# The input product of the last batch: four of eight pairs of ff tiles by seven block products, seeded and summed through PSUM

## The chip, the cores and the metric

The kernel runs on one core of one Trainium2 chip. The metric is the device time of one execution in microseconds (us); the time of the kernel before is the median of three executions. A core has five engines with instruction streams of their own: TensorE (PE in the profile, with its weight loads as PEld), VectorE (DVE), ScalarE (ACT), GpSimd (POOL) and SyncE (SP, which here only issues transfers). Matmuls read on-chip memory (SBUF) and write PSUM, which has eight banks of 512 fp32 columns for each of 128 partitions.

## What is computed

A block-sparse attention, whose output is the input of a two-layer network with a sigmoid-approximated gelu between the layers:

```python
def _moe_ref(x, w_in, w_out):
    h = x @ w_in                                  # [3072, 512] @ [512, 2048]
    g = h * (1.0 / (1.0 + np.exp(-1.702 * h)))
    return (g @ w_out).astype(np.float32)         # [3072, 2048] @ [2048, 512]

def reference(**kwargs):
    ...
    attn_out = _attn_ref(**attn_kwargs)           # 4 batches, 8 heads, 768 positions, 64 wide
    x = attn_out.transpose(0, 2, 1, 3).reshape(B * S, H * D)
    return _moe_ref(x=x, **moe_kwargs)
```

The change concerns `h = x @ w_in` and the gelu of the last batch only.

## The kernel before

A batch of 768 tokens is worked as two *units* of 384 tokens (`HALF`). Unit `u` of batch `b` is `2*b` or `2*b + 1`; the last batch (`b = 3`) has units 6 and 7. The hidden dimension of 2048 is 16 *ff tiles* of 128 (`NT = 16`), and `NI = 8` pairs of them. For each ff tile the input product takes four matmuls (`KO = 4` pieces of the 512-wide contraction) into a PSUM bank, and ACT writes the gelu of it to `gT`.

All operations of an engine are kept in program order by a wrapper (`_Ordered`), so an operation that waits holds up all later ones of its engine.

```python
psb = ctx.enter_context(tc.tile_pool(name="psb", bufs=2, space=bass.MemoryType.PSUM))   # tag "big": 2 x 2 banks
pmm = ctx.enter_context(tc.tile_pool(name="pmm", bufs=4, space=bass.MemoryType.PSUM))   # tag "mm": 4 x 1 bank
...
xTT = [[keep.tile([128, 2, HALF], F16, name=f"xT{m}{g}") for g in range(2)] for m in range(2)]
xT = [[xTT[m][p // 2][:, p % 2] for p in range(NP)] for m in range(2)]
gT = [keep.tile([128, NT, HALF], F16, name=f"gT{s}") for s in range(2)]
...
def ff_in(u, nts):
    phs = [pmm.tile([128, HALF], F32, name="ph", tag="mm") for nt in nts]
    for k0 in (0, 2):
        for nt, ph in zip(nts, phs):
            for ko in (k0, k0 + 1):
                pe.matmul(out=ph, lhsT=w_in_sb[:, ko, nt * 128:(nt + 1) * 128],
                          rhs=xT[u % 2][ko], start=(ko == 0), stop=(ko == KO - 1))
    for nt, ph in zip(nts, phs):
        act.activation(out=gT[u % 2][:, nt, :], in_=ph, func=ACT.Gelu_apprx_sigmoid)
```

The output product `g @ w_out` of a batch already uses seven products in place of eight, on pairs of token tiles: pair a is two token tiles of the first unit, b is one of each unit, c is two of the second. `sums` makes the sums of quarters that the seven products need; it reads and updates `gT` on DVE, for pairs `i0` to `i1` of ff tiles.

```python
def sums(self, i0, i1):                      # in class Pair
    i = slice(i0, i1)
    dve.tensor_add(self.s1[:, i], self.a21[:, i], self.a22[:, i])
    dve.tensor_sub(self.s2[:, i], self.s1[:, i], self.a11[:, i])
    dve.tensor_sub(self.a21[:, i], self.a11[:, i], self.a21[:, i])

def p1(self, eng=dve):
    self.x = bank("px")                      # bank(): a tile of pmm, tag "mm"
    product(self.x, self.a11, ts["b11"], True)
    self.t1 = held(self.x, eng)
def p6(self):
    product(self.x, self.s2, ts["t2"], False)
    self.t2 = held(self.x, act)
    dve.tensor_sub(self.s2, self.a12, self.s2)
def p7(self):
    self.w = bank("pw")
    product(self.w, self.a21, ts["t3"], True)
def p2(self):
    y = bank("py")
    product(y, self.a12, ts["b21"], True)
    dve.tensor_add(self.osb(0)[:, 0:DH], y[:, 0:DH], self.t1)
    self.store(0, 0, False)
# ... p3, p4, p5 in the same manner
order = ["a7", "a2", "a6", "b1", "a5", "b7", "a3", "a4", "b6", "b2", "b5",
         "c1", "b3", "c7", "c6", "c2", "c5", "b4", "c3", "c4"]
```

The end of the loop over batches (cut to what the last batch does):

```python
for b in range(1, B):
    n, s = b + 1, (b + 1) % 2
    more = n < B
    u = 2 * b
    # ... pairs a, b, c
    first, second = {}, {0: [lambda: pairs["a"].sums(0, NI)]}
    for nt, i0, i1 in ((7, 0, 4), (13, 4, 7)):
        second[nt] = [lambda i0=i0, i1=i1: pairs["b"].sums(i0, i1),
                      lambda i0=i0, i1=i1: pairs["c"].sums(i0, i1)]
    # ... what the earlier batches do beside the input product
    for w, todo in ((u, first), (u + 1, second)):
        ff_in(w, range(3))
        for nt in range(NT):
            if nt > 2:
                ff_in(w, (nt,))
            for f in todo.get(nt, ()):
                f()
    pairs["a"].p1(act)
    # ...
    for m in "bc":
        pairs[m].sums(NI - 1, NI)
    for what in order:
        getattr(pairs[what[0]], "p" + what[1])()
        # ... attention of the next batch between, if there is one
```

Of the kernel before, what the change touches and what calls it, by code (L numbers as in the profile page):

```python
# [9 lines left out]
F32 = mybir.dt.float32  # L10
BF16 = mybir.dt.bfloat16
F16 = mybir.dt.float16
AX = mybir.AxisListType
ALU = mybir.AluOpType
ACT = mybir.ActivationFunctionType
# [20 lines left out]
def kernel(  # L36
# [10 lines left out]
    B, H, S, D = q.shape  # L47
# [10 lines left out]
    KO = d_model // 128  # L58
    NT = d_ff // 128
    HALF = S // 2  # L60
# [3 lines left out]
    pe = _Ordered(tc, nc.tensor)  # L64
    dve = _Ordered(tc, nc.vector)
    act = _Ordered(tc, nc.scalar)
# [5 lines left out]
    stage = ctx.enter_context(tc.tile_pool(name="stage", bufs=1))  # L72
    castp2 = ctx.enter_context(tc.tile_pool(name="cast2", bufs=1))
    attp = ctx.enter_context(tc.tile_pool(name="att", bufs=4))
    outp = ctx.enter_context(tc.tile_pool(name="outp", bufs=4))
    psb = ctx.enter_context(tc.tile_pool(name="psb", bufs=2, space=bass.MemoryType.PSUM))
    pmm = ctx.enter_context(tc.tile_pool(name="pmm", bufs=4, space=bass.MemoryType.PSUM))
# [3 lines left out]
    raw, early = {}, {}  # L81
# [60 lines left out]
    def v_odd(b):  # L142
        for p in range(NP):
            r = rows_of(b % 2, p)
            dve.tensor_copy(out=r[:, :, 1], in_=r[:, :, 0])
# [87 lines left out]
# [3 lines that stand above are left out]
    w_in_sb = keep.tile([128, KO, d_ff], F16, name="w_in_sb")  # L236
# [38 lines left out]
    def copy(eng, out, in_):  # L275
        if eng is act:
            act.activation(out=out, in_=in_, func=ACT.Copy)
        elif eng == "dve_alone":

            dve.tensor_reduce(out=out, in_=in_.unsqueeze(len(in_.shape)), axis=AX.X, op=ALU.max)  # L280
        else:
            eng.tensor_copy(out=out, in_=in_)
# [58 lines left out]
    def block_sums():  # L341
        for g in range(4):
            dve.tensor_copy(out=vs[0:32, 2 * g:2 * g + 2, 0:D],
                            in_=vs_ps[0][32 * g:32 * g + 32, :]
                            .rearrange("p (h d) -> p h d", d=D))


    def halo_dmas(w5, j0):
        halo_odd(w5, j0)
        halo_even(w5, j0)  # L350
# [220 lines left out]
    def tk(p, s):  # L571
        ps = trans(rows["k", 1][:, p].rearrange("p j h d -> p j (h d)"))
        copy(dve, at(flat_kx(p, s), 0, [[256, NJ], [192, 2], [1, 64]]),
             ps.rearrange("p (j e c) -> p j e c", e=2, c=64))
        ks = attp.tile([128, nb], BF16, name="ks", tag="ks")
        dve.tensor_reduce(out=ks, in_=ps.rearrange("p (n s) -> p n s", s=block),
                          axis=AX.X, op=ALU.max)
        key_halos(p, s)
        key_rows(p, s, ks)
# [3 lines left out]
    def xk(g, b):  # L583
        s = b % 2
        k4 = kxs[s].rearrange("p i (j e) c -> p (i j) e c", e=2)
        src = rows["k", b][:, 2 * g:2 * g + 2].rearrange("p i j h d -> p (i j h d)")
        for e in range(2):
            sp.dma_start(out=k4[:, 2 * g * NJ:2 * (g + 1) * NJ, e, e * 64:e * 64 + 64],
                         in_=src[e * 64:e * 64 + 64], transpose=True)
# [7 lines left out]
    def rest_k(p, s):  # L597
        ks = attp.tile([128, nb], BF16, name="ks", tag="ks")
        dve.tensor_reduce(out=ks.rearrange("p (j e n) -> p j e n", e=2, n=2),
                          in_=at(flat_kx(p, s), 0, [[256, NJ], [192, 2], [block, 2], [1, block]]),  # L600
                          axis=AX.X, op=ALU.max)
        key_halos(p, s)
        key_rows(p, s, ks)
# [4 lines left out]
    a_sb, x_sb, x2 = {}, {}, {}  # L608
# [11 lines left out]
    def values(b, half, g, big=False):  # L620

        pvs = []
        for i in range(2):
            p = 2 * g + i
            a = a_sb[p]
            if big and i == 0:
                ps = psb.tile([128, 1024], F32, name="ps_av", tag="big")
            one = (ps[:, i * 512:i * 512 + 512] if big else
                   pmm.tile([128, 512], F32, name="ps_av", tag="mm"))
            pv = one[:, 0:390].rearrange("p (h j c) -> p h j c", h=2, j=JH)  # L630
            pvs.append(pv)
            for hh in range(2):
                for j in range(JH):
                    for e in range(2):
                        t = 2 * j + e
                        pe.matmul(out=pv[e * 64:e * 64 + 64, hh, j, :], lhsT=a[:, hh, t, :],
                                  rhs=vw[b % 2][:, half * TH + t, 2 * p + hh, 0:D + 1],
                                  start=True, stop=True, skip_group_check=True)
        x2[g] = attp.tile([128, 2, JH, 2, D], F16, name="x2", tag="x2")
        for i in range(2):  # L640
            norm(x2[g][:, i], pvs[i])
# [15 lines left out]
    def dx(g, m):  # L657
        sp.dma_start(out=xTT[m][g].rearrange("p i (j c) -> p (i j) c", c=128),
                     in_=x2[g].rearrange("p i j h d -> p (i j h d)"), transpose=True)
# [17 lines left out]
    def ff_first(p):  # L677
# [6 lines left out]
        if len(seen) == KO:  # L684
            for nt in range(N0):
                act.activation(out=gT[0][:, nt, :], in_=ph0[nt], func=ACT.Gelu_apprx_sigmoid)

    po_now = {}

    def ff_out(u, ms, part):  # L690
# [12 lines left out]
    NI, DH = NT // 2, d_model // 2  # L703
# [265 lines left out]
    for u in range(2):  # L969
        todo = {}  # L970
# [3 lines left out]
        else:  # L974
            def value_rows():
# [7 lines left out]
            todo = {0: [lambda: tk(0, 1)], 3: [lambda: tk(1, 1)], 5: [lambda: v_odd(1)],  # L983
                    6: [lambda: tk(2, 1)], 9: [value_rows], 11: [lambda: tk(3, 1)]}
# [45 lines left out]
# [3 lines that stand above are left out]
        ss = stage.tile([128, NP - 1, 2, NI, 128], F16, name="ss", tag="vf")  # L1033
        u = 2 * b
        pairs = {"a": Pair((u, 0), (u, 1), ss[:, 0], not more),
                 "b": Pair((u, 2), (u + 1, 2), ss[:, 1], not more),
                 "c": Pair((u + 1, 0), (u + 1, 1), ss[:, 2], not more)}
# [4 lines that stand above are left out]
        if b == 1:  # L1042
            first = {0: [lambda: values(1, 1, 0, True)], 2: [lambda: dx(0, 1), lambda: values(1, 1, 1, True)],
                     4: [lambda: dx(1, 1)]}
        elif more:
            for g in range(2):
                xk(g, n)
        if more:
            first.setdefault(6, []).append(lambda: v_odd(n))
            at_k = [(first, 3), (first, 5), (first, 8), (first, 10)] if b == 1 else \  # L1050
                [(first, 8), (first, 10), (first, 12), (first, 14)]
            for p, (when, nt) in enumerate(at_k):
                when.setdefault(nt, []).append(lambda p=p: rest_k(p, s))

            def bring():
                w5 = vw[s].rearrange("p (j e) h c -> p j e h c", e=2)
                vsum(s, range(NJ))
                block_sums()
                halo_dmas(w5, 0)
                sum_dmas(w5, 0)  # L1060

            def later():
                pool.tensor_copy(out=after, in_=ss[:, 2, 0, 0, 0:2])
                load_kc(n + 1)
                load_vc(n + 1)
                load_qc(n + 1)

            if n + 1 < B:
                second[7].append(later)
            when = 7 if b == 1 else 14  # L1070
            first.setdefault(when, []).append(lambda: [xq(g, n) for g in range(2)])
            first.setdefault(9 if b == 1 else 15, []).append(bring)
        for w, todo in ((u, first), (u + 1, second)):
            ff_in(w, range(3))
            for nt in range(NT):
                if nt > 2:
                    ff_in(w, (nt,))
                for f in todo.get(nt, ()):
                    f()
        pairs["a"].p1(act)  # L1080
        if more:
            exp_soon()
        for m in "bc":
            pairs[m].sums(NI - 1, NI)
        for what in order:
            getattr(pairs[what[0]], "p" + what[1])()
            if more:
                for it in meet.get(what, ()):
                    attend(n, it)
# [30 lines left out]
```

## Time and profile before

| | |
|---|---|
| device time | 212.51 us (211.75 to 213.37) |
| span of the profiled execution | 210.6 us |
| mean granted TensorE clock | 1.000 |
| input products, all batches | 512 matmuls of 384 columns, 86.2 us |
| gelus, all batches | 128 on ACT, 60.9 us, mean 490 ns |
| input product of the last batch | 168.10 to 188.90 us |
| output products of the last batch | from 188.90 us, the last begins at 206.37 |

In the timeline each line is a run of like instructions: start and length in us, engine, operation, what it writes and reads, how many; in brackets how long the engine stood idle before it, and whose end released it. `ph` is a bank of the input product, `px`, `pw` and `py` are banks of the output product, `ss` the sums. All operations go through one helper, so they all have its line number, and groups are told apart by the names of their tiles. A table of windows gives, for each stretch of time, its length, the busy time of PE, PEld, DVE, ACT and POOL with the number of instructions, the granted clock, the share of the transfer engines and GB/s.

### The profile page before, as it was taken

The numbers are of one execution on the slowest core, as the hardware profiler recorded it, in microseconds if no ns is written. First come the engines' busy times: TensorE is split into PE (matmuls) and PEld (weight loads), VectorE is DVE, ScalarE is ACT, GpSimd is POOL, SyncE is SP. The second block draws the span as 40 slices with busy tenths as digits, with TensorE's granted clock in tenths as the row PEclk, the third lists the DMA queues.
The fourth block names the chain that finished last, engine by engine and source line by source line (L and its number), as shares of the span: only waits on it lengthen the run. The fifth ranks groups of instructions, "written<-read, shape, count | busy, mean of one in ns | idle before, by whom it ended". The sixth has DMA issues, their size and how long they took to land.

```text
span 210.6 us, 5499 instructions
## 1 busy us (share of the span) xinstructions
PE 201.3 (96%) x2193; PEld 137.1 (65%) x2193; DVE 133.0 (63%) x394; ACT 122.0 (58%) x228; POOL 95.0 (45%) x173
## 2 busy tenths in 40 slices
PE   7879999999999999989999989999999999999993
PEld 2667565556665666556888856557888856668882
DVE  6487956587946669936767860797757710366332
ACT  2674878156685488667744557677444667772220
POOL 8788989699897943425998120220000000000000
PEclk9999999999999999999999999999999999999999
DMA  5999999999998999999999999995043250000223
GB/s 160 302 159 205 241 244 221 175 152 224 167 136 164 131 113 211 157 142 122 167 132 200 177 214 157 174 98 63 3 137 90 72 155 0 3 0 25 84 77 117
DMA packets 96609, 29.33 MB, mean 139 GB/s; under 512 B 84480, under 2 KB 93600, under 8 KB 96584
## 3 DMA queue, kind: packets, MB, share of 16 engines
q0 software_dynamic: 67920, 14.88, 81.9%
q1 hardware_dynamic: 28664, 14.11, 34.2%
q8 instruction: 17, 0.28, 0.6%
q14 instruction: 8, 0.07, 0.1%
HBM read 27.26 MB, written 6.29 MB: 159 GB/s over the span
## 4 chain that ended last, share of the span: by engine, by line
PE 81%; DMA 10%; DVE 3%; POOL 2%; issue 1%; SPq 0%
PE ph L28 36%; PE px L28 14%; PE po L28 10%; DMA xT<-x 8%; PE pw L28 7%; PE ps_av L28 4%; PE py L28 3%; PE ps_s L28 3%; DMA kf<-in_k_dram 2%; POOL vb L28 2%; DVE qT L28 1%; PE ps_t L28 1%; PE ps_x L28 1%; PE ps_q L28 1%; DVE x_sb L28 1%
## 5 line engine op out<-in xcount | busy, mean ns | idle before, releaser
L28 PE MATMUL ph<-xT,w_in_sb 128*128 128x384 f16 x512 | 86.2, 326 | 1.6 <-DMA xT<-x 1.5
L28 ACT ACTIVATE gT<-ph 128x384 f16<-128x384 f32 x128 | 60.9, 490 | 27.2 <-PE ph L28 27.0
L28 PEld LDWEIGHTS <-w_in_sb 128*128 128x128 f16 x512 | 49.4, 98 | 34.0 <-issue 2.2
L28 PEld LDWEIGHTS <-gT 128*128 128x128 f16 x384 | 35.6, 98 | 12.4
L28 ACT ACTIVATE a_sb<-ps_s 128x768 bf16<-128x768 f32 x28 | 21.2, 806 | 11.6 <-PE ps_s L28 11.6
L28 PE MATMUL po<-w_out_sb,gT 128*128 128x512 f16 x96 | 23.1, 380 | 0.0
L28 PEld LDWEIGHTS <-ss 128*128 128x128 f16 x216 | 21.0, 98 | 2.5
L28 DVE TENSOR_TENSOR a_sb<-a_sb,mk 128x768 bf16<-128x768 bf16 x28 | 15.6, 557 | 10.0 <-ACT a_sb L28 8.4
L28 DVE TENSOR_TENSOR ss<-gT 128x512 f16<-128x512 f16 (+3 forms) x21 | 8.0, 381 | 21.4 <-ACT gT L28 21.4
L28 ACT ACTIVATE t<-px 128x256 f32<-128x256 f32 x21 | 8.1, 384 | 20.2 <-PE px L28 20.2
L28 PE MATMUL pw<-tb,gT 128*128 128x256 f16 x144 | 18.7, 273 | 0.0
L28 PE MATMUL px<-ta,ss 128*128 128x256 f16 x144 | 18.7, 273 | 0.0
L28 DVE TENSOR_REDUCE ks<-kx 128x24 bf16<-128x768 bf16 x12 | 11.3, 944 | 7.9 <-DMA kx<-kb 7.9
L28 DVE TENSOR_TENSOR x<-ps_av,rc 128x384 f16<-128x384 f32 x28 | 15.6, 558 | 1.0
L28 POOL DMA_DIRECT2D vw<-in_v_dram x18 | 15.9, 938 | 0.3 <-DMA kq<-in_k_dram 0.3
L28 POOL DMA_DIRECT2D vw<-vw x12 | 6.8, 585 | 19.9 <-DVE vw L28 10.2
L28 POOL DMA_DIRECT2D kb<-in_k_dram x16 | 13.2, 863 | 2.0 <-DMA w_out_sb<-in_moe_w_out_dram 1.6
L28 POOL DMA_DIRECT2D qb<-in_q_dram x16 | 13.3, 914 | 1.0 <-DMA vw<-in_v_dram 1.0
L28 DVE TENSOR_TENSOR osb<-pw,t 128x256 f32<-128x256 f32 x18 | 7.6, 423 | 9.2 <-PE pw L28 5.1
L28 ACT ACT_TABLE_LOAD x10 | 12.8, 1283 | 1.0 <-PEq L1104 0.8
L28 ACT ACTIVATE osb<-px 128x256 f32<-128x256 f32 x9 | 3.4, 379 | 12.0 <-PE px L28 12.0
L28 DVE RECIPROCAL rc<-ps_av 128x6 f32<-128x6 f32 x32 | 6.0, 188 | 6.6 <-PE ps_av L28 6.3
(103 smaller groups left out, 253.7 us busy)
## 6 DMA issues: line engine op xcount, KB each, us to landing
out_dram<-osb SPq DMA_DIRECT2D x18, 256.0 KB, 5.2
vw<-in_v_dram POOLq DMA_DIRECT2D x18, 128.0 KB, 6.0
w_in_sb<-in_moe_w_in_dram POOLq DMA_DIRECT2D x4, 512.0 KB, 8.5
w_out_sb<-in_moe_w_out_dram POOLq DMA_DIRECT2D x4, 512.0 KB, 16.0
kf<-in_k_dram SPq DMA_DIRECT2D x8, 192.0 KB, 4.7
kb<-in_k_dram POOLq DMA_DIRECT2D x16, 96.0 KB, 4.8
qb<-in_q_dram POOLq DMA_DIRECT2D x16, 96.0 KB, 7.5
out_dram<-osb SPq DMA_DIRECT2D x12, 128.0 KB, 1.7
```

Of the source, the lines that this page charges most:

```text
L28: r = f(*a, **kw)
```

## The change

In the last batch, the input product of ff tiles 8 to 15 is taken, for both units at once, as four pairs of ff tiles. For one pair, the 2x2 blocks are: weights by ff tile (even, odd) and half of the contraction, and x by half of the contraction and unit. Their product needs seven block products in place of eight, with four sums of weight blocks (`wsum`, made on DVE during batch 2) and four differences of x blocks (`xsum`, made on DVE in batch 3). The intermediate sums are built in PSUM: a product is copied by DVE into a second bank and matmuls go on accumulating onto both; or DVE adds a held product to a bank and writes the result to another bank, onto which matmuls accumulate. The aim is to give TensorE eight block matmuls fewer per two units in this part. Tiles 0 to 7 of both units stay as they were, those of unit 7 placed between the pairs; in unit 6 they are spread over all eight PSUM banks. The sums of pairs a, b and c for the output product move: a in two steps, one before and one after the pairs, b and c wholly after.

```diff
+    WI = 4
+    wt = {}
+    def win_weights(i0, i1):
+        if i0 == 0:
+            w = w_in_sb.rearrange("p k (i e c) -> p e k i c", e=2, c=128)[:, :, :, NI - WI:]
+            wt.update({(e, h): w[:, e, 2 * h:2 * h + 2] for e in range(2) for h in range(2)})
+            wt["s"] = stage.tile([128, 4, 2, WI, 128], F16, name="wsum", tag="kf")
+        o, i = [wt["s"][:, n, :, i0:i1] for n in range(4)], slice(i0, i1)
+        a11, a12, a21, a22 = (wt[e, h][:, :, i] for e in range(2) for h in range(2))
+        dve.tensor_add(o[0], a21, a22)
+        dve.tensor_sub(o[1], o[0], a11)
+        dve.tensor_sub(o[2], a11, a21)
+        dve.tensor_sub(o[3], a12, o[1])
+
+    def ff_in_pairs(u, early):
+        (b11, b21), (b12, b22) = xTT
+        xs = castp2.tile([128, 4, 2, HALF], F16, name="xsum", tag="kb")
+        t = [xs[:, n] for n in range(4)]
+        big = [psb.tile([128, 1024], F32, name="pw_in", tag="big") for _ in range(2)]
+        mm = [pmm.tile([128, 512], F32, name="px_in", tag="mm") for _ in range(4)]
+        X = [big[0][:, 0:HALF], big[1][:, 0:HALF], mm[0][:, 0:HALF]]
+        V = [b[:, 512:512 + HALF] for b in big]
+        Y = [m[:, 0:HALF] for m in mm[1:3]]
+        L = mm[3][:, 0:HALF]
+        # ... gelu(w, f, src): ACT, to gT; one(w, f, ps): four matmuls and the gelu of one ff tile
+        def prod(ps, a, b, i, first=False):
+            for k in range(2):
+                pe.matmul(out=ps, lhsT=a[:, k, i], rhs=b[:, k], start=(first and k == 0), ...)
+        def A(i):
+            x, v, y = X[i % 3], V[i % 2], Y[i % 2]
+            prod(x, wt[0, 0], b11, i, True)
+            dve.tensor_copy(out=y, in_=x)
+            prod(v, ws[2], t[2], i, True)
+            hold[i] = attp.tile([128, HALF], F32, name="m7", tag="x2")
+            copy(act, hold[i], v)
+        def Bp(i):
+            x, v, y = X[i % 3], V[i % 2], Y[i % 2]
+            prod(x, ws[1], t[1], i)
+            dve.tensor_add(v, x, hold[i])
+            prod(y, wt[0, 1], b21, i)
+            gelu(u, f0(i), y)
+        def C(i):
+            x, v = X[i % 3], V[i % 2]
+            prod(x, ws[0], t[0], i)
+            c = attp.tile([128, HALF], F32, name="c22", tag="a_sb")
+            dve.tensor_add(c, x, hold[i])
+            prod(v, wt[1, 1], t[3], i)
+            gelu(u, f0(i) + 1, v)
+            gelu(u + 1, f0(i) + 1, c)
+        def Dp(i):
+            x = X[i % 3]
+            prod(x, ws[3], b22, i)
+            gelu(u + 1, f0(i), x)
+        free = [X[0], X[1], X[2], V[0], V[1], Y[0], Y[1], L]
+        for f in range(2 * (NI - WI)):
+            one(u, f, free[f % 8])
+        early()
+        for n, (x, y) in ((2, (b22, b12)), (0, (b12, b11)), (1, (b22, t[0])), (3, (b21, t[1]))):
+            dve.tensor_sub(t[n], x, y)
+        rest = list(range(2 * (NI - WI)))
+        for i in range(WI + 1):
+            if i < WI:
+                A(i)
+            if i:
+                C(i - 1)
+            one(u + 1, rest.pop(0), L)
+            if i < WI:
+                Bp(i)
+            if i:
+                Dp(i - 1)
+            if i < WI - 1:
+                one(u + 1, rest.pop(0), L)
 ...
+        if b == B - 2:
+            for n0 in range(WI):
+                first.setdefault(n0, []).append(lambda n0=n0: win_weights(n0, n0 + 1))
+        if not more:
+            ff_in_pairs(u, lambda: pairs["a"].sums(0, NI - WI))
-        for w, todo in ((u, first), (u + 1, second)):
+        for w, todo in ((u, first), (u + 1, second)) if more else ():
 ...
-        for m in "bc":
-            pairs[m].sums(NI - 1, NI)
+        if more:
+            for m in "bc":
+                pairs[m].sums(NI - 1, NI)
+        else:
+            pairs["a"].sums(NI - WI, NI)
+            for m in "bc":
+                pairs[m].sums(0, NI)
```

More of the change, by code (lines that the diff above doesn't have):

```diff
@@ new lines, in ff_in_pairs, with gelu, one, f0 @@
+    def ff_in_pairs(u, early):
[8 more added lines that the diff above has]
+        L = mm[3][:, 0:HALF]
+        def gelu(w, f, src):
+            act.activation(out=gT[w % 2][:, f, :], in_=src, func=ACT.Gelu_apprx_sigmoid)
+        def one(w, f, ps):
+            for ko in range(KO):
+                pe.matmul(out=ps, lhsT=w_in_sb[:, ko, f * 128:(f + 1) * 128], rhs=xT[w % 2][ko],
+                          start=(ko == 0), stop=(ko == KO - 1))
+            gelu(w, f, ps)
+        def prod(ps, a, b, i, first=False):
+            for k in range(2):
+                pe.matmul(out=ps, lhsT=a[:, k, i], rhs=b[:, k], start=(first and k == 0),
+                          stop=(k == 1), skip_group_check=True)
+        ws = [wt["s"][:, n] for n in range(4)]
+        hold = {}
+        def A(i):
[23 more added lines that the diff above has]
+            gelu(u + 1, f0(i), x)
+        def f0(i):
+            return 2 * (NI - WI + i)
+        free = [X[0], X[1], X[2], V[0], V[1], Y[0], Y[1], L]
[17 more added lines that the diff above has]
+                one(u + 1, rest.pop(0), L)
+        assert not rest
```

## The prediction

> **What bounds the kernel now.** I read the page's table of engines first, then the groups, and then went through the last batch in the timeline, with a table of windows beside it.
>
> ```profile
> PE 201.3 (96%) x2193; PEld 137.1 (65%) x2193; DVE 133.0 (63%) x394; ACT 122.0 (58%) x228; POOL 95.0 (45%) x173
> ```
>
> TensorE (PE) has work 96% of the span, so time is won only by giving it fewer instructions, and lost whenever it waits. The timeline of the last batch shows where the change lies (start, length, engine, operation, idle time before it):
>
> ```profile
> 168.10 20.96 PE L28 MATMUL ph<-xT,w_in_sb 128*128 128x384 f16 x128
> ...
> 173.50 0.49 ACT L28 ACTIVATE gT<-ph 128x384 f16<-128x384 f32 x1 [0.16 <-PE ph L28]
> ...
> 179.23 0.69 DVE L28 TENSOR_TENSOR ss<-gT 128x1024 f16<-128x1024 f16 x1 [10.08 <-ACT gT L28]
> 179.95 0.69 DVE L28 TENSOR_TENSOR ss<-ss,gT 128x1024 f16<-128x1024 f16 x1
> ...
> 184.43 0.43 DVE L28 TENSOR_TENSOR ss<-gT 128x512 f16<-128x512 f16 x1 [3.18 <-ACT gT L28]
> 184.89 0.43 DVE L28 TENSOR_TENSOR ss<-ss,gT 128x512 f16<-128x512 f16 x1
> 185.23 0.42 DVE L28 TENSOR_TENSOR gT<-gT,gT 128x512 f16<-128x512 f16 x1
> ...
> 188.90 1.04 PE L28 MATMUL px<-w_out_sb,gT 128*128 128x256 f16 x8
> ```
>
> The input product of units 6 and 7 is one unbroken run of 128 matmuls. The next product starts at 188.90, so one matmul costs (188.90 - 168.10)/128 = 0.1625 us. ScalarE (ACT) takes 0.49 us for each gelu and waits 0.16 us between two; VectorE (DVE) idles 10.08 us in this stretch. The windows of the stage confirm it (length, then the busy time of each engine):
>
> ```profile
> 168.00:173.30 5.30, 5.30 (x35) 3.22 (x33) 1.11 (x4) 3.22 (x8) 0.00 (x0) 1.00 0.60 186
> 173.30:178.50 5.20, 5.20 (x34) 3.13 (x32) 0.00 (x0) 3.92 (x9) 0.00 (x0) 1.00 0.00 0
> 178.50:188.90 10.40, 10.40 (x66) 6.26 (x64) 4.81 (x11) 7.62 (x17) 0.00 (x0) 1.00 0.01 2
> ```
>
> PE is full in all three. Whatever waits the change puts into this stretch are a direct loss.
>
> [...] here four gelus in a row take 1.79 us, that is (1.79 - 0.49)/3 = 0.433 us apart, an overlap of 0.06.
>
> **What it removes.** Eight ff tiles of each unit stay direct: 64 matmuls. The other 64 become 4 pairs x 7 products x 2 halves of the contraction = 56, all of 384 columns. PE gets 120 in place of 128: 8 x 0.1625 = **1.30 us** less. That is the whole possible gain, 0.6%.
>
> **What it adds.** In batch 2, 16 small DVE operations of 256 fp16 elements for the weight sums. Between the measured 0.22 us (128) and 0.36 us (384) I estimate 0.29 us each, 4.6 us. DVE is idle from 124.9 to 132.9 there, waiting for a transposed load, so they cost nothing. In batch 3: four differences of 768 elements of x (0.557 us, from the bf16 multiply of the same size), and per pair a copy PSUM to PSUM, two additions with a PSUM operand (each about 0.56 us, from x<-ps_av of 384), and one more ACT copy (about 0.49). The pair stage holds 88 matmuls, 14.3 us of PE, against 28 ACT operations, 28 x 0.433 to 0.49 = 12.1 to 13.7 us, and 12 DVE operations, 6.7 us. Throughput is enough; the question is order.
>
> **The first wait.** Each engine runs in program order. DVE gets early(), the three sums of pair a over tiles 0 to 7, ahead of the four differences, and these sums need the gelu of tile 7, the last direct one. I set out from the old timeline. PE starts at 168.10; tile 1 goes to the second large PSUM buffer, which the last values of batch 3 free only when DVE's normalisation ends at 168.81, so PE loses about **0.2**. The 32 direct matmuls then end at 168.10 + 0.2 + 5.2 = 173.5. The gelu starts 0.2 later (in before, the last: 189.10 against 188.90) and ends at 174.19. DVE starts early() at 174.23; three sums of 512 take 185.56 - 184.43 = 1.13, so the first difference, t2, runs from 175.36 to 175.92. PE meanwhile has only the two matmuls of product 1, until 173.83; its next one multiplies by t2 and starts at about 175.98. Loss **2.15 us**.
>
> **The second wait.** PE then does the two of product 7 and one direct tile of unit 7: 176.0 + 6 x 0.1625 = 176.98. The next adds s1*t1 onto product 1, and must wait until DVE has copied product 1 out. DVE's order: t0 at 175.83, t1 at 176.41, t3 at 177.0, copy at 177.47 to 178.03. PE resumes at 178.1. Loss **1.1 us**.
>
> **The steady loop.** One round has 22 matmuls, 3.58 us. The bank L serves two direct tiles per round. Between the end of one and the start of the next are 6 matmuls, 0.98 us, in which its gelu must be through. ACT at that time has a hold copy and the two gelus of the round before in front of it. By hand, at 0.433 us apart, the gelu of L ends 1.0 to 1.1 us after the tile: about 0.1 us lost in each of two rounds. At the end C(3) follows D(2) with no tile between, and its addition onto x must wait for DVE's v addition: about 0.2. Together **0.4 us**.
>
> **The end.** The sums of b and c, formerly spread over the second unit, now all run after the last gelu. DVE: six operations of 1024 elements, at the old spacing (0.72 + 0.61 + 0.60) x 2 = 3.86 us. Product 1 of pair a starts by the terms above at 188.90 - 1.30 + 0.2 + 2.15 + 1.1 + 0.4 = 191.45; the last gelu ends at about 192.85, so the sums end at about 196.75 and p2's addition at 197.15. There are four product banks. a7, a2, a6, b1 and a5 take 0.87 us each; b7 needs a fifth and can only take p2's, at about 197.2, while PE is ready at 191.45 + 6 x 0.87 = 196.7. Loss **0.45 us**. a7 itself does not wait: the sums over tiles 8 to 15 end before its fifth matmul.
>
> **Sum.** -1.30 + 0.2 + 2.15 + 1.1 + 0.4 + 0.45 = **+3.0 us**: 212.51 + 3.0 = **215.5 us**, 1.4% slower.
>
> **Rivals.** (1) *All hidden.* If the four differences did not sit behind early(), they would be done long before: their inputs land by 172.0, where the DMA share falls to 0. Then 1.30 comes off and about 1.0 of small waits goes on: 212.2. For it speaks DVE's long idle time; against it the fixed order, so it needs a mistake of mine. (2) *ACT becomes the bound.* If copies and gelus of the pair stage run at 0.49 and never back to back, and the c gelus wait for DVE each time, every round loses 0.3 to 0.5 us, 1.5 us more in all: 217. For it: 28 operations in a stage of 15 us; against it: measured gelus do run at 0.433 when queued. (3) *The clock falls* after two stalls within 5 us. [...] so I hold it unlikely. (4) *Buffers come in another order*: should the first tile get the later large buffer, 0.65 us more; should product 1 of pair a get L's bank, it waits for the last gelus, up to 0.8 us more. Then 216 to 217.
>
> **Range and chances.** The two big terms rest on program order and measured lengths, each good to some 0.4 us. Rivals 2 to 4 lie above and only 1 below, so the range is 214.2 to 217.2. The bound for slower by 2% is 216.8, reached with a rival added: 0.16. Faster by 2% would need 208.3, more than the whole removal: 0.01. Within 2%: 0.83.
>
> **What would show it.** Right: 120 matmuls in the input product of the last batch; a PE gap of about 2 us near 174 to 176, released by DVE's t2, and one of about 1 us near 177 to 178, released by the copy; then small gaps by gelu; product 1 of pair a near 191.5; a gap of about 0.4 before b7. Wrong: no gap at 174 (the order isn't what I think), gaps in every round (ACT binds), or PEclk below 9.

## The result, and the profile after

The changed kernel takes **221.58 us** (median of six; 220.94 to 222.54) where the kernel before takes 212.99 beside it: a ratio of 1.041, with a 95% interval of 1.036 to 1.046. The prediction was 215.5, with a range to 217.2.

| | before | after |
|---|---|---|
| first matmul of the last input product to product 1 of pair a | 168.10 to 188.90: 20.80 us | 168.99 to 198.33: 29.34 us |
| from there to the end of the span | 21.74 us | 21.76 us |
| PE busy in the span | 201.3 us (96%) | 204.5 us (93%) |
| mean granted TensorE clock | 1.000 | 0.974 |

I call the first row *the stage*. The whole loss lies in it: 8.54 of some 8.6 us. The profiled run of the changed kernel also reaches it 0.9 us late, after a stretch of half clock from 17.5 to 20.9 us, far ahead of anything changed; lengths of the stage leave that out.

Below, `x`, `y`, `v` and `L` are the banks of the diff, A to D the blocks of a pair; product 1 is the first into `x` and product 7 the one into `v`, both in block A; a direct tile is one of ff tiles 0 to 7, taken as before; the pair stage is what follows the direct tiles of unit 6. The timeline of the changed kernel, in the same columns as before, around the start of the pair stage:

```profile
168.99 1.59 PE L28 MATMUL pw_in<-xT,w_in_sb 128*128 128x384 f16 x8
...
174.32 0.49 PE L28 MATMUL pw_in<-xT,w_in_sb 128*128 128x384 f16 x2
...
175.04 0.42 DVE L28 TENSOR_TENSOR ss<-gT 128x512 f16<-128x512 f16 x1 [5.01 <-ACT gT L28]
...
176.17 1.02 DVE L28 TENSOR_TENSOR xsum<-xT,xT 128x768 f16<-128x768 f16 x2
177.23 1.15 DVE L28 TENSOR_TENSOR xsum<-xT,xsum 128x768 f16<-128x768 f16 x2
178.30 0.56 DVE L28 COPY px_in<-pw_in 128x384 f32<-128x384 f32 x1
178.91 0.80 PE L28 MATMUL pw_in<-xsum,wsum 128*128 128x384 f16 x2 [4.10 <-DVE px_in L28]
```

DVE's order is as I had it: three early sums, four differences, then the copy of product 1. But product 7, on the last line, starts after the *copy*, at 178.91, and not after the first difference, ready at 176.7. Further on, the waits that return:

```profile
184.84 0.81 PE L28 MATMUL pw_in<-xsum,wsum 128*128 128x384 f16 x4 [0.66 <-DVE px_in L28]
...
186.31 0.48 PE L28 MATMUL pw_in<-xsum,w_in_sb 128*128 128x384 f16 x2 [0.65 <-DVE c L28]
...
189.23 0.81 PE L28 MATMUL pw_in<-xsum,wsum 128*128 128x384 f16 x4
...
190.69 0.48 PE L28 MATMUL pw_in<-xsum,w_in_sb 128*128 128x384 f16 x2 [0.65 <-DVE c L28]
...
194.43 0.48 PE L28 MATMUL pw_in<-xsum,w_in_sb 128*128 128x384 f16 x2
```

Product 7 of the second pair waits for the copy too; that of the third (189.23) does not. The v product of block C waits for `c` in the first two pairs, and not in the third (194.43). In the first two pairs x and v are the halves of one two-bank tile (`X[0]`, `V[0]` in `big[0]`; `X[1]`, `V[1]` in `big[1]`); in the third and fourth they are in different tiles. The windows (length, busy time of the five engines, then granted clock, transfer share, GB/s) show the second surprise:

```profile
174.00:176.00 2.00, 0.81 (x5) 0.38 (x4) 0.93 (x3) 0.85 (x2) 0.00 (x0) 1.00 0.00 0
176.00:178.00 2.00, 0.00 (x0) 0.00 (x0) 1.93 (x5) 0.00 (x0) 0.00 (x0) 0.97 0.00 0
178.00:180.00 2.00, 1.09 (x4) 0.56 (x4) 0.86 (x2) 0.26 (x1) 0.00 (x0) 0.50 0.00 0
180.00:182.00 2.00, 2.00 (x8) 0.91 (x6) 0.26 (x1) 0.72 (x2) 0.00 (x0) 0.50 0.00 0
182.00:184.00 2.00, 2.00 (x7) 0.91 (x6) 0.30 (x1) 0.91 (x2) 0.00 (x0) 0.50 0.00 0
184.00:186.00 2.00, 1.00 (x5) 0.39 (x4) 0.87 (x2) 0.56 (x2) 0.00 (x0) 0.82 0.00 0
186.00:188.00 2.00, 1.69 (x11) 1.04 (x11) 0.38 (x2) 1.17 (x3) 0.00 (x0) 1.00 0.00 0
```

From about 177.9 to 184.7 PE has half its clock. PE is "busy" there, but a matmul takes 0.32 us in place of 0.1625: the six that start at 181.42 end where the next starts, at 183.34.

### The profile page after: what moved, and what is told of

Read it like the earlier page. It is cut to its first block, busy times and chain, and to the rows that moved or that the text cites. A ratio compares the mean times of both kernels' runs of the same rounds, so it can differ in the third digit from the quotient of the medians.

```text
span 220.1 us, 5530 instructions
## 1 busy us (share of the span) xinstructions
PE 204.5 (93%) x2185; PEld 138.2 (63%) x2185; DVE 145.8 (66%) x417; ACT 123.2 (56%) x232; POOL 94.6 (43%) x173
## 2 busy tenths in 40 slices
DMA packets 96610, 29.34 MB, mean 133 GB/s; under 512 B 84480, under 2 KB 93600, under 8 KB 96584
## 4 chain that ended last, share of the span: by engine, by line
PE 69%; POOL 12%; DMA 7%; DVE 7%; SPq 2%; issue 2%; ACT 0%; DVEq 0%; POOLq 0%
PE ph L28 20%; PE px L28 14%; PE pw L28 8%; PE px_in L28 5%; PE pw_in L28 5%; PE po L28 5%; PE py L28 4%; DMA kb<-in_k_dram 3%; PE ps_s L28 3%; PE ps_av L28 3%; POOL mk L28 2%; POOL kb L28 2%; POOL qb L28 2%; DMA qf<-in_q_dram 2%; DMA qb<-in_q_dram 2%; SPq L28 2%
## 5 line engine op out<-in xcount | busy, mean ns | idle before, releaser
L28 PEld LDWEIGHTS <-w_in_sb 128*128 128x128 f16 x472 | 46.0, 99 | 32.9 <-issue 4.5
L28 PE MATMUL ph<-xT,w_in_sb 128*128 128x384 f16 x384 | 65.0, 326 | 0.0
L28 ACT ACTIVATE gT<-ph 128x384 f16<-128x384 f32 x96 | 45.6, 490 | 21.0 <-PE ph L28 20.8
L28 DVE TENSOR_TENSOR ss<-gT 128x512 f16<-128x512 f16 (+3 forms) x18 | 7.5, 418 | 9.9 <-ACT gT L28 9.9
L28 PE MATMUL px_in<-xT,w_in_sb 128*128 128x384 f16 x58 | 13.2, 360 | 0.0
```

The costliest lines, as they stand in the source:

```text
L28: r = f(*a, **kw)
```

## The experiments

The theory after the result: two causes on top of the predicted ones. A matmul into one half of a two-bank PSUM tile waits for DVE or ACT still at work on the other half (4.10 us for product 7 of the first pair, 0.66 for that of the second); and the idle gap lets the clock fall (to 0.50, from 177.89 to 184.71). The rivals: DVE's order alone; or ACT and DVE can't keep up with the pair stage at all.

Lengths of the stage from the profile of each run, times as medians, ratios to the kernel before with the 95% interval:

| kernel | stage, us | time, us | ratio |
|---|---|---|---|
| before | 20.80 | 212.7 to 213.2 in the four comparisons | 1 |
| changed | 29.34 | 221.58 | 1.041 (1.036 to 1.046) |
| e1: buffers | 25.78 | 217.69 | 1.021 (1.015 to 1.026) |
| e2: DVE order | 24.87 | 218.81 (216.5 to 222.0) | none given |
| e9: the same again | 24.54 | 216.53 | 1.015 (1.010 to 1.020) |
| e3: 22 idle matmuls | 26.91 | 219.38 | 1.031 (1.024 to 1.038) |
| e6: 11 idle matmuls | 28.19 | 220.21 | 1.036 (1.031 to 1.041) |
| e4: buffers and order | 21.43 | 213.40 | 1.001 (0.999 to 1.004) |
| e10: the same again | 21.42 | 213.81 | 1.000 (0.997 to 1.004) |
| e5: more moved | 21.68 | 215.26 | 1.010 (1.007 to 1.014) |
| e7: side works alone | 20.80 | 212.74 | 0.999 (0.996 to 1.001) |
| e8: neighbours and queue | 20.46 | 212.99 | 0.997 (0.994 to 0.9997) |

The remainder of the span after the stage is 21.7 to 21.8 us in all of them but e5 (22.4).

### e1: x and v of a pair in different tiles

```diff
-        X = [big[0][:, 0:HALF], big[1][:, 0:HALF], mm[0][:, 0:HALF]]
-        V = [b[:, 512:512 + HALF] for b in big]
-        Y = [m[:, 0:HALF] for m in mm[1:3]]
+        X = [m[:, 0:HALF] for m in mm[0:3]]
+        V = [b[:, 0:HALF] for b in big]
+        Y = [b[:, 512:512 + HALF] for b in big[::-1]]
```

> Only the PSUM buffers are dealt out anew: the three x banks and L are single-bank tiles, each v bank shares a large tile with the y bank of the other parity. If the waits for DVE's copy (4.1 and 0.7 us) and for c (0.7 us, twice) come from x and v of one pair lying in one two-bank tile, they go, and the first gap splits: about 2.0 us until the first difference is ready, one direct tile, then about 1.2 us until the copy. [...] if the clock falls only for one long idle piece it stays at 1.0 and the time is 216.0 (210 + 6); if a low share of work over several us is enough, it still falls to 0.5 and the time is 218.5. Rival, throughput of ACT and DVE: the waits only move, 220 to 221.

The waits of PE in that part of the profile (who waited for whom: us in total, times, longest):

```profile
PE pw_in L28 <- DVE xsum L28: 2.0, 1, 2.0
PE px_in L28 <- DVE pw_in L28: 1.0, 1, 1.0
PE pw_in L28 <- ACT gT L28: 0.6, 1, 0.6
```

The gap splits as the prediction had it in the first place: 2.0 us for the first difference, 1.0 for the copy (predicted 2.15 and 1.1). The waits for `c` are gone. The stage loses 3.56 us, so the two-bank tile is a cause, and the rival "throughput" falls. Still, the clock fell, for one stretch of 3.4 us (179.16 to 182.58):

```profile
178.00:180.00 2.00, 1.14 (x5) 0.64 (x5) 1.30 (x3) 0.41 (x1) 0.00 (x0) 0.79 0.00 0
180.00:182.00 2.00, 2.00 (x8) 0.91 (x6) 0.08 (x2) 0.98 (x2) 0.00 (x0) 0.50 0.00 0
182.00:184.00 2.00, 2.00 (x12) 1.13 (x11) 1.12 (x2) 1.15 (x3) 0.00 (x0) 0.86 0.00 0
```

The time lies between my two figures for clock held and clock fallen, 216.0 and 218.5. The last wait, 0.6 us for a gelu, is new: in this deal two direct tiles of unit 6 in a row lie in one large tile.

### e2: the differences of x ahead of the direct tiles

```diff
+        for n, (x, y) in ((2, (b22, b12)), (0, (b12, b11)), (1, (b22, t[0])), (3, (b21, t[1]))):
+            dve.tensor_sub(t[n], x, y)
         for f in range(2 * (NI - WI)):
             one(u, f, free[f % 8])
-        early()
-        for n, (x, y) in ((2, (b22, b12)), (0, (b12, b11)), (1, (b22, t[0])), (3, (b21, t[1]))):
-            dve.tensor_sub(t[n], x, y)
 ...
                 Bp(i)
+            if i == 0:
+                early()
```

> Only the order on DVE is changed: the four differences of x before the direct tiles, the early sums of pair a after the first block B. If the long gap is DVE's order, it shrinks from 4.1 to about 0.6 us (the copy of product 1 alone), the clock stays at 1.0, and 3.5 + 2.5 us come off: 215.5. The waits of one tile (0.7 us, three times) stay. Rival, the gap is set by something else (the large tile's release, the throughput of ACT): 220 or more.

```profile
173.30 1.03 DVE L28 TENSOR_TENSOR xsum<-xT,xT 128x768 f16<-128x768 f16 x2 [3.74 <-DMA xT<-x]
174.36 1.15 DVE L28 TENSOR_TENSOR xsum<-xT,xsum 128x768 f16<-128x768 f16 x2
175.43 0.56 DVE L28 COPY px_in<-pw_in 128x384 f32<-128x384 f32 x1
...
177.69 0.57 DVE L28 TENSOR_TENSOR pw_in<-pw_in,m 128x384 f32<-128x384 f32 x1 [1.71 <-ACT gT L28]
```

The gap shrinks from 4.1 to 1.7 us, not to 0.6: the differences now wait for the transfer of x itself, which lands only at 173.30, 4.8 us after the stage begins, and the copy stands behind them. The clock stays at 1.0 in the stage and 4.5 us come off it. So DVE's order is a cause as well, and neither of the two is enough alone.

```profile
168.00:193.00 25.00, 20.89 (x125) 11.86 (x123) 11.33 (x23) 15.64 (x35) 0.00 (x0) 1.00 0.13 40
```

Two of the four executions, 220.77 and 221.98, lay well above the other two, which left too few for a ratio, so I ran the same kernel once more.

> The second experiment once more, whose four times lay at 216.5, 216.9, 220.8 and 222.0. With idle pieces of 1.7, 1.0 and twice 0.65 us in 7 us it is near the point at which the clock falls: [...] the times form two groups, about 216.7 and about 3 to 5 us above. If the spread was of another kind, they form one group.

Six times from 215.1 to 217.3, one group, with the clock at 1.0 in the profiled stage again. The guess of two groups was not borne out; what raised the two times in the first run stays open. The mean clock of one of these two, 220.77, was 1.000, so no fall of the clock raised that one.

### e3 and e6: the gap filled with idle matmuls

```diff
             dve.tensor_copy(out=y, in_=x)
+            for _ in range(22 if i == 0 else 0):       # e6: 11
+                pe.matmul(out=Y[1], lhsT=wt[0, 0][:, 0, 0], rhs=b11[:, 0], start=True,
+                          stop=True, skip_group_check=True)
             prod(v, ws[2], t[2], i, True)
```

> 22 idle matmuls of 384 columns (3.6 us), whose result is overwritten, fill the long gap; the waits are those of the changed kernel. If the fall of the granted clock to 0.5 for some 7 us is due to the idle gap and costs about 2.5 us in the 16 to 20 matmuls that run then, plus longer waits, the time falls to 218.5 to 219. Rival, the clock falls for another reason or its fall costs nothing because the pair stage waits for ACT and DVE anyway: 221.5.

This is the direct measure of the clock. With 22 idle matmuls product 7 still waits for the copy, and the waits of 0.66 and twice 0.65 us remain, but the clock reads 1.00 all through, behind the former gap too:

```profile
178.00:180.00 2.00, 1.47 (x10) 0.78 (x8) 0.99 (x2) 0.43 (x1) 0.00 (x0) 1.00 0.00 0
182.00:184.00 2.00, 0.81 (x4) 0.38 (x4) 1.05 (x2) 0.58 (x2) 0.00 (x0) 1.00 0.00 0
```

The clock held, and the stage is 29.34 - 26.91 = **2.43 us** shorter, with 3.6 us more work in it. The time falls by 2.2. The rival, that a fallen clock costs nothing because PE waits anyway, is out for these two profiled executions. In single times the price is not resolved: three of the six executions of the changed kernel have a mean clock of 0.992. One stretch of 3.4 us at half clock takes 0.008 off the mean of 220 us, so there was room for one and not for two, and they took 220.9 to 221.6 us, hardly less than the other three (221.5 to 222.5).

> As the third experiment with 11 idle matmuls in place of 22: 1.8 us of the 4.1 us gap filled, 2.3 us idle. [...] If, as the first experiment suggests (2.0 and 1.0 us idle, clock at 0.5 for 3.3 us), [...] it may fall for one such stretch: 1.5 us more, 221.

With 11 of them the idle piece is 2.3 us, followed by the wait of 0.66:

```profile
PE pw_in L28 <- DVE px_in L28: 3.0, 2, 2.3
PE pw_in L28 <- DVE c L28: 1.3, 2, 0.6
```

The clock fell from about 179.7 to 183.1, one stretch of 3.4 us, and cost 28.19 - 26.91 = 1.28 us. So one idle piece of 2.3 us was followed by a fall as well:

```profile
179.00:180.00 1.00, 1.00 (x6) 0.49 (x5) 0.00 (x0) 0.82 (x2) 0.00 (x0) 0.85 0.00 0
180.00:181.00 1.00, 1.00 (x5) 0.48 (x4) 0.57 (x1) 0.43 (x1) 0.00 (x0) 0.50 0.00 0
```

It was not so in every execution: one of the other three, 220.36, has a mean clock of 1.000.

### e4: buffers and order together

The edits of e1 and e2 in one kernel.

> Both the buffers of the first and the order of the second experiment. If these two are the causes, all that is left is the removal of 1.3 us and small waits (copy of product 1 none, 0.1 to 0.2 per round): 212 to 213, level with the kernel before. Rival, throughput of ACT and DVE in the pair stage: 215 or more, with gaps in each round that ACT releases.

```profile
PE pw_in L28 <- ACT gT L28: 0.6, 1, 0.6
PE pw_in L28 <- DVE pw_in L28: 0.3, 1, 0.3
```

```profile
178.67 0.42 DVE L28 TENSOR_TENSOR gT<-gT 128x512 f16<-128x512 f16 x1
179.00 0.56 DVE L28 COPY pw_in<-px_in 128x384 f32<-128x384 f32 x1
...
179.61 0.49 PE L28 MATMUL pw_in<-xsum,w_in_sb 128*128 128x384 f16 x2 [0.28 <-DVE pw_in L28]
```

The view lists two waits, 0.58 us for a gelu as in e1, and 0.28 us of block C's `v` product for a copy into the other half of its large tile, which stands behind the early sums in DVE's queue. The clock reads 1.0; the stage is 21.43 us and the time level with before. Of the changed kernel's excess of 8.54 us in the stage, 7.9 are gone by two edits that leave every product, copy and sum in place. As 120 matmuls need 19.5 us, 1.9 us are left over and eat the removed 1.30: counted from start to start the two waits are 0.74 and 0.44 us, and five gaps of 0.1 to 0.24 us make up the rest.

> The fourth experiment again beside the eighth, on the same chip: 213.3, level with before; the eighth is 0.4% under it if its waits are gone.

The repeat gave 213.81 (ratio 1.000) and a stage of 21.42.

### e7: the side works alone

```diff
         if not more:
-            ff_in_pairs(u, lambda: pairs["a"].sums(0, NI - WI))
-        for w, todo in ((u, first), (u + 1, second)) if more else ():
+            second = {0: [lambda: pairs["a"].sums(0, NI)]}
+        for w, todo in ((u, first), (u + 1, second)):
 ...
-            pairs["a"].sums(NI - WI, NI)
             for m in "bc":
                 pairs[m].sums(0, NI)
```

> The input product of the last batch as before, direct, but with the change's two side works: the 16 weight sums in batch 2 (whose result is not used) and the sums of pairs b and c wholly after the last gelu. By the prediction the first costs nothing and the second 0.45 us: 213.6; by the trace of the changed kernel the second costs nothing either: 213.2. Rival, the side works hold part of the loss: 214 or more.

Here the input product is the direct one, and the weight sums are made for nothing. Stage 20.80 us, the rest 21.74, time 0.999 of before: the 16 weight sums in batch 2 and the late sums of b and c cost nothing that shows.

### e5 and e8: the small waits

e5 is e4 with three more edits, e8 with the first two of them and one difference moved:

```diff
-        free = [X[0], X[1], X[2], V[0], V[1], Y[0], Y[1], L]
+        free = [X[0], X[1], V[0], V[1], X[2], Y[1], Y[0], L]      # e5, e8
 ...
-            if i == 0:
-                early()
+            if i < WI:
+                early(i)                                         # e5, e8: one pair of ff tiles at a time
 ...
             dve.tensor_add(c, x, hold[i])
+            one(u + 1, rest.pop(0), L)                           # e5 only: ahead of the v product
             prod(v, wt[1, 1], t[3], i)
 ...
                 A(i)
+            if i == 0:
+                dve.tensor_sub(t[3], b21, t[1])                  # e8 only: behind the copy of product 1
             if i:
                 C(i - 1)
-            one(u + 1, rest.pop(0), L)
+            else:                                                # e5 only
+                one(u + 1, rest.pop(0), L)
```

> On top of the fourth experiment: the direct tiles of unit 6 visit the banks in an order in which no two neighbours lie in one large tile; the early sums of pair a go one pair of ff tiles at a time behind each block B; and in block C a direct tile of unit 7 stands between the x product and the v product. If what was left there (0.58, 0.28 and 0.1 to 0.2 us per round) comes from neighbours in one tile and from DVE's queue, the stage shrinks from 21.4 to about 20.1 us, and the time comes to 0.6% below the fourth experiment, 212.2 where the kernel before has 213.2. Rival, ACT and DVE bind the rounds: the stage stays at 21 or more and the time level with before.

A miss: 215.26, worse than e4 and than the rival's figure, which was level with before. With the direct tile ahead of the v product, the gelu of v comes later, and the next y product, whose bank lies in the same large tile, waits for it:

```profile
PE pw_in L28 <- ACT gT L28: 0.9, 3, 0.3
PE px_in L28 <- DVE pw_in L28: 0.5, 1, 0.5
PE pw L28 <- DVE gT L28: 0.3, 1, 0.3
```

The third line is product 7 of pair a, which now waits for sums that came later with the gelus. The waits were moved, not removed. In the profile the stage is 0.25 us and the rest 0.65 us longer than in e4. The ratios lie 0.9% apart, some 1.9 us; the other 1 us is not explained, and the profiled execution was the slowest of the ten (218.05).

> The fourth experiment with less moved than in the fifth: direct tiles of unit 6 never on two neighbouring halves of one large tile, the last difference of x behind the copy of product 1, the early sums of pair a one pair at a time behind each block B; block C as in the change. Left of the fourth experiment's waits should be the 0.1 to 0.2 us per round: stage 20.5 us where the fourth has 21.4 and before has 20.8; time 0.4% under the fourth experiment and 0.2 to 0.4% under before, 212.3. Rival, each wait taken away comes back as another (as in the fifth experiment): 213.3 or more.

The windows of e8, direct tiles of unit 6 and pair stage:

```profile
169.10:174.60 5.50, 5.50 (x36) 3.33 (x34) 1.92 (x6) 3.53 (x8) 0.00 (x0) 1.00 0.58 176
174.60:189.56 14.96, 14.87 (x88) 8.37 (x86) 9.97 (x28) 12.04 (x27) 0.00 (x0) 1.00 0.01 2
```

The stage is 20.46 us, 0.97 under e4 and 0.34 under before, as expected (20.5): about a fourth of the 1.30 us that the seven products save. The time is 212.99, where e4's repeat beside it has 213.81; the ratio to before is 0.997, with an interval that ends at 0.9997. So it is at best just faster than before, and 212.3 was not reached. PE is busy 14.87 of the 14.96 us of the pair stage, ACT 12.0 and DVE 10.0, so neither of these two binds.

## Why the prediction was wrong

By its own steps, in us on the stage of the changed kernel:

| step | predicted | measured |
|---|---|---|
| eight matmuls removed | -1.30 | -1.30 (120 matmuls, 19.5 us at full clock) |
| second large buffer late | +0.2 | +0.13 |
| first wait and second wait | +2.15 + 1.1 | +4.27 in one piece |
| steady loop: small waits | +0.4 | about +0.5 |
| steady loop: waits for the copy and c | not there | 0.86 + 0.82 + 0.81 = +2.5 |
| fall of the clock | a rival, "unlikely" | +2.4 to 2.5 |
| end, b7's bank | +0.45 | +0.02 |
| sum | +3.0 | +8.6 |

How the measured ones are worked out: the direct tiles and product 1 end at 174.32 + 2 x 0.1625 = 174.64, and product 7 starts at 178.91. The 16 matmuls from 178.91 to 183.98 take 5.07 us in place of 2.60. The waits for the copy and `c` are the starts 184.84, 186.31 and 190.69 less the end of PE's work before them (183.98, 185.49, 189.88). The small waits are what remains of 29.34. The gap of 4.27 is longer than the 4.10 in the bracket of the trace, since its bracket counts from the modelled end of the matmul.

**Right:** the matmuls removed, at 0.1625 us each (the run of 128 of before took 20.80 us); that program order on DVE puts early() ahead of the differences (the three sums and four differences run at the predicted lengths); that the weight sums cost nothing that shows (e7); that ACT and DVE have the throughput (e8: busy for 12.0 and 10.0 of 14.96 us).

**Wrong, first step:** "PE meanwhile has only the two matmuls of product 1, until 173.83; its next one multiplies by t2 and starts at about 175.98." I looked at the operand of product 7 and not at its target. The target shares a tile with product 1, and the matmul waited for DVE's copy of product 1. That merged two waits with work between them into one idle piece of over 4 us, a whole us longer than their sum. The same oversight left out 2.5 us in the loop. The prediction treated the eight banks as eight buffers; they were four of one bank and two of two. Natural evidence was in the trace after (pairs one and two wait, three and four do not), and e1 shows it: with x and v in different tiles, the first two waits come out at 2.0 and 1.0.

**Wrong, second step:** rival 3, the fall of the clock, "so I hold it unlikely." The trace of before did not show what lets the clock fall: it was 1.00 throughout. I reckoned with two stalls; merged, they were one of 4.27 us, and the clock fell to 0.50 for 6.8 us. In e1 two pieces of 2.0 and 1.0 us, in e6 one of 2.3, were followed by a fall too, of 3.4 us. e3 puts its price in the changed kernel at 2.43 us. Nor was the first step alone what put the number out: in e1 the two waits came as predicted, and its 217.69 is still above the range, with one stretch of half clock and a new wait for a gelu.

**Mis-sized, end:** b7 did not wait for p2's bank. The last gelu ended 0.9 us after product 1 of pair a began (199.20 against 198.33), not 1.4, so DVE's sums, which run ahead of p2's addition, were through in time: p2's addition ends at 203.54 and b7 starts at 203.59, which is when PE is free.

**Rival 1** assumed x landed by 172.0, where the transfer engines fall idle in the profile of before. In e2 the transfer engines fall idle at about 172.5 and DVE's wait for x ends at 173.30, 0.8 us later and 4.8 us after the stage began. "Done long before" was too hopeful; with the right order the differences and the copy behind them follow the landing of x.

What stays open: whether the tile-wide wait is needed by anything on the chip. No run here tried the two halves without the wait, as the program's tracking of buffers sets it. I only dealt the buffers out differently (0.66 us for product 7 of the second pair with x and v in one tile, no wait in e1 with them in two).

## What to carry to other kernels

Before counting on overlap in PSUM, list for each matmul not only its operands but what shares the *tile* of its target: a two-bank tile was one buffer here, and a copy out of one half held up the matmul into the other (0.66 us in the second pair of the changed kernel). Put the work that opens the next stage ahead of work that only closes a later one in an in-order queue: most of the long gap went once the early sums stood behind the differences, and they still cost a wait of 0.28 us in e4, where another copy stood behind them. Where PE is the bound, an idle gap can cost more than its length (4.27 us of gap brought a fall of the clock to 0.50 here, which cost 2.43 us more), and an algebraic saving of 1.3 us needs every chain behind it planned to a few tenths: after all repairs, a fourth of it was left.

## What the runs showed of the hardware that was not expected

The prediction held a fall of the clock unlikely, and the trace of before, at 1.00 throughout, showed none. After the change the granted clock fell to 0.5 and stayed there for 3.4 us (e1: 179.16 to 182.58; e6: 179.71 to 183.12) or 6.8 us (changed: 177.89 to 184.71). The idle pieces before were 2.0 and 1.0 us with six matmuls, 0.98 us, between (e1), 2.3 us (e6) and 4.1 us (changed). With pieces of 1.7 and 1.0 us and 16 matmuls, 2.6 us, between (e2), of 1.4 and 1.0 us with the same 16 between (its repeat), and of 0.53, 0.66 and 0.65 us (e3) the clock in the profiled stage stayed at 1.0.

Nor did the fall begin at one time after the gap: in the changed kernel it came at 177.89, while PE still stood idle (174.64 to 178.91); in e1 at 179.16 and in e6 at 179.71, 0.3 and 1.4 us after PE had taken up work again (178.86 and 178.32). What decides whether and when the clock falls was not shown: no run moved a gap on purpose, and of the executions of e6 the profiled one had a fall in the stage and another, of 220.36 us, a mean clock of 1.000.
